# One attention kernel, fewer products against the maximum: key differences in a shared PSUM pair

## The chip, the cores and the metric

The program runs on one NeuronCore of a Trainium2 chip, in one launch. The metric is device time in microseconds (us) of one execution; less is better. In the rows PE is the matrix engine (PEld its weight loads), DVE the vector engine, ACT the scalar engine, POOL is GpSimd, and SP issues DMAs (SPq, ACTq: DMA issues on these queues).

## What is computed

Attention with queries averaged in pairs, then a gated layer and a soft mixture of experts. Cut to what matters here:

```python
# q, k, v: (4, 8, 1152, 64)
q_pool = q.reshape(B, H, S // 2, 2, D).mean(axis=3)          # 576 queries
scores = scale * np.matmul(q_pool, k.transpose(0, 1, 3, 2))  # 576 x 1152
scores = scores - np.max(scores, axis=-1, keepdims=True)
attn = np.exp(scores); attn = attn / (np.sum(attn, axis=-1, keepdims=True) + 1e-09)
attn_out = np.matmul(attn, v)
h = x @ w_in; x = (h * np.cos(h)) @ w_out                    # 2304 tokens, 512 -> 2048 -> 512
# then: logits, two softmaxes, 8 experts with 4 slots each, combined per token
```

The change touches the attention alone (and the moments at which some weights of the gated layer are decoded beside it).

## The kernel before

**Attention.** Two of the 32 heads make a pair; a pair fills the 128 partitions (64 per head). There are 16 pairs, and each has two units of 288 queries. A unit has nine score blocks, one for every 128 keys. A block t goes through these steps:

- *products* (L409): fp32 matmuls of the keys `kr` and pooled queries `qs` into a PSUM pair `s` (two banks, [128, 2, 512]), then *maxima* (L418): four bf16 matmuls of ones with `D`, a matrix that has minus the maximum of each query on its diagonals. They subtract the maximum from the scores in PSUM;
- *exp* (L423, ACT), from PSUM to an `e` buffer in SBUF;
- *av* (L431, PE): `e` times the values `vr`, added up over the nine blocks in the PSUM pair `o`;
- *add* (L440): `e` is added to a running sum, on DVE (letter V in `ADD_BY`) or on GpSimd (G). The first block of each letter is only the start. So a unit has three additions on DVE and four on GpSimd, and one (L443, DVE) that joins the two sums. Then `sums` (L511, PE), and a chain of small DMAs (L526, L536, L540), a reciprocal (L529) and a scaling on GpSimd (L543, L555).

The maxima come from a coarser product: 14 *rounds* per pair (L305, PE, bf16) into PSUM, each reduced by DVE (L310), then a small turn (L317), a last reduction (L324, L329) and nine diagonals on ACT (L343). They are made one pair ahead. Per pair SP loads `qr` (both queries of each average), `kr`, `vr`; DVE averages (L260, as a sum: the factor sits in the exponent's scale); ACT casts to bf16 (L263).

**PSUM.** Three pairs of banks (`BANKS = 3`) serve the score blocks, the rounds and the sums; a user takes whichever is free first. The fourth pair is `o`.

**Order.** Every step is entered into `Plan` with an engine, a duration and a due time; `Plan.order` lists them: each engine takes, of the steps that can start first, the one that is due first. Due times are multiples of `P` plus numbers of the tables `ROUNDS` and `DUES`. A step with `port=True` is kept from overlapping with another such step (DVE additions and GpSimd's work). So each engine's order is fixed when the program is built, and on the chip an engine waits at an instruction until its operands are there; nothing behind it passes.

Of the kernel before, what the change touches and what calls it, by code (L numbers as in the profile page):

```python
# [135 lines left out]
class Attention:  # L136
# [15 lines left out]
    ROUNDS = (-10.7, -8.2, -10.4, -9.8, -3.7, -4.8, -3.3, -0.8, -8.1, 0.5, 1.6, 2.2, 7.5, 7.7)
    FIRST_ROUNDS = (-13, -12, -11, -10, -9, -8, -7, -5, -7.2, -4.0, -2.3, -1.6, 0.9, 2.4)
    E_BUFS = 8

    BEHIND = 13.8
# [72 lines left out]
    def operands(self, p, m):  # L229
# [40 lines left out]
        for i, (a, n) in enumerate(q_parts):  # L270
            x = op(m + 0.5 * i, "SP", 0.6, lambda a=a, n=n: load_q(a, n), [first], uses=[("qr", p)],
                   more=4.2 if p else (2.4, 2.8, 3.3)[i], early=early)
            x = op(at_("pooled", 0.1 * i) if p else m, "V", 0.07 + n / 960, lambda a=a, n=n: pooled(a, n), [x], uses=[("qr", p), ("qs", p)], port=True)
# [1245 lines left out]
```

## Time and profile before

| what | us |
|---|---|
| runs: median (lowest, highest) of 3 | 871.1 (870.7, 872.5) |
| the profiled execution: its own time | 872.76 |
| its span, first to last instruction | 870.5 |
| attention, first round to last av | 7.5 to 398 |
| PE, DVE, ACT, POOL busy, share of the span | 97%, 81%, 61%, 45% |

The attention takes the first 45% of the span, the gated layer and the experts the rest. A busy share is an average over stages; matmul rows show modelled ends, so that what a group of matmuls costs is read from its start to the start of the next group. The granted TensorE clock is full (1.00) in all stretches of the attention.

### The profile page before, as it was taken

The page shows a single profiled execution, that of the slowest core. Times are in us where ns is not written, and L with a number is a line of the kernel's source. Part 1 is how long each engine was busy: PE and PEld are TensorE (multiplying, and loading weights), DVE is VectorE, ACT ScalarE, POOL GpSimd, SP SyncE. Part 2 cuts the span into 40 slices and gives each one's busy share as a digit, 9 for nine tenths or more (in the row PEclk, how much of TensorE's full clock was granted, in tenths as well). Part 3 has the DMA queues.
Part 4 walks back from the last instruction along what each step waited for, and adds up shares of the span by engine and source line. Part 5 has one row for each costly group of instructions (what it writes and reads, how often), then busy time and mean ns, then how long its engine had stood idle before and what let it go on. Part 6 is the DMA issues. An engine that isn't in the chain of part 4 may idle for free.

```text
span 870.5 us, 24363 instructions
## 1 busy us (share of the span) xinstructions
PE 847.4 (97%) x9901; PEld 612.2 (70%) x9901; DVE 704.2 (81%) x1309; ACT 527.7 (61%) x1132; POOL 390.6 (45%) x381
## 2 busy tenths in 40 slices
PE   5999999999999999999999999999999999999996
PEld 3666566656666666667788888888888888877355
DVE  6999999899899888855989888888899889544423
ACT  3777777767777777774875555555555555454223
POOL 0566656766666666664554333344433333220100
PEclk9999999999999999999999999999999999999898
DMA  7033323333333233111121111110111110594897
GB/s 254 15 94 113 112 74 90 98 106 101 101 101 88 80 101 101 46 44 44 54 61 50 36 37 49 49 48 29 49 49 49 38 36 13 226 422 151 317 423 227
DMA packets 53969, 90.89 MB, mean 104 GB/s; under 512 B 21473, under 2 KB 33505, under 8 KB 49761
## 3 DMA queue, kind: packets, MB, share of 16 engines
q1 hardware_dynamic: 53568, 88.76, 31.3%
q8 instruction: 77, 1.26, 0.6%
q10 hardware_dynamic: 288, 0.59, 0.2%
q14 instruction: 36, 0.29, 0.1%
HBM read 78.71 MB, written 4.72 MB: 96 GB/s over the span
## 4 chain that ended last, share of the span: by engine, by line
PE 91%; DVE 4%; ACT 2%; issue 1%; POOL 1%; DMA 1%; SPq 0%; DVEq 0%; ACTq 0%
PE ops L780 21%; PE hps L780 21%; PE o L431 16%; PE s L409 15%; PE m L305 4%; PE s L418 4%; PE hq L1341 2%; PE so L1384 2%; PE sums L511 1%; DVE mp L310 1%; PE xtp L961 1%; PE fo L1413 1%; DMA qr<-in_q_dram 1%; PE lgp L975 1%; PE sps L1160 1%
## 5 line engine op out<-in xcount | busy, mean ns | idle before, releaser
L310 DVE TENSOR_REDUCE mp<-m 128x2 f32<-128x768 f32 x224 | 203.6, 952 | 29.8 <-PE m L305 29.4
L423 ACT ACTIVATE e<-s 128x576 f32<-128x576 f32 x288 | 176.3, 653 | 53.2 <-PE s L418 50.7
L780 PE MATMUL ops<-w,g 128*128 128x512 f32 x864 | 206.3, 391 | 2.0 <-POOL g L818 1.4
L780 PE MATMUL hps<-x,w 128*128 128x512 f32 (+1 forms) x960 | 204.5, 368 | 0.0
L780 PEld LDWEIGHTS hps<-x,w 128*128 128x128 f32 x960 | 168.0, 188 | 31.7 <-issue 1.5
L780 PEld LDWEIGHTS ops<-w,g 128*128 128x128 f32 x864 | 160.7, 188 | 36.9 <-POOL g L818 2.4
L409 PE MATMUL s<-qs,kr 64*64 64x288 f32 x2304 | 180.5, 403 | 3.2 <-DVE mp L310 3.1
L431 PE MATMUL o<-e,vr 64*64 64x288 f32 x2304 | 181.0, 406 | 0.0
L818 POOL TENSOR_TENSOR g<-r,g 128x512 fp32r<-128x512 f32 (+1 forms) x80 | 100.1, 1252 | 147.3 <-ACT g L815 121.3
L440 POOL TENSOR_TENSOR acc<-acc,e 128x576 f32<-128x576 f32 x96 | 136.6, 1423 | 3.2 <-ACT e L423 0.9
L805 ACT ACTIVATE r<-r 128x512 f32<-128x512 f32 (+1 forms) x160 | 94.0, 587 | 69.4 <-DVE r L798 67.7
L440 POOL TENSOR_TENSOR acc<-e 128x576 f32<-128x576 f32 x32 | 48.5, 1517 | 153.5 <-ACT e L423 153.5
L409 PEld LDWEIGHTS s<-qs,kr 64*64 64x64 f32 x2304 | 79.7, 133 | 44.0 <-DVE mp L310 7.4
L431 PEld LDWEIGHTS o<-e,vr 64*64 64x64 f32 x2304 | 82.7, 133 | 31.8 <-issue 7.1
L741 POOL TENSOR_TENSOR da<-da,w 128x256 f32<-128x256 f32 x64 | 49.3, 771 | 94.6 <-DVE db L730 42.1
L418 PE MATMUL s<-D,a_ones 64*64 64x288 bf16 x1152 | 87.2, 283 | 0.0
L305 PE MATMUL m<-kb,qb 64*64 64x384 bf16 x896 | 74.0, 331 | 9.3 <-ACT qb L263 7.5
L798 DVE SCALAR_TENSOR_TENSOR r<-ki,hps 128x512 f32<-128x512 int32 (+1 forms) x80 | 50.4, 631 | 36.1 <-ACT ki L795 34.1
L815 ACT CAST g<-r 128x512 fp32r<-128x512 f32 (+1 forms) x80 | 46.2, 578 | 40.0 <-DVE r L808 37.5
L795 ACT ACTIVATE ki<-hps 128x512 int32<-128x512 f32 (+1 forms) x80 | 44.0, 551 | 39.1 <-PE hps L780 38.0
L941 DVE TENSOR_TENSOR acc<-acc,ops 128x512 f32<-128x512 f32 x70 | 47.7, 685 | 22.4 <-PE ops L780 22.4
L343 ACT ACTIVATE D<-a_minus,mc 128x64 bf16<-128x64 f32 x142 | 37.4, 336 | 33.1 <-DVE mc L324 32.9
(148 smaller groups left out, 952.5 us busy)
## 6 DMA issues: line engine op xcount, KB each, us to landing
raw<-in_w_io_dram SPq DMA_DIRECT2D x64, 256.0 KB
w1t<-in_w_dram SPq DMA_DIRECT2D x15, 1024.0 KB
vr<-in_v_dram SPq DMA_DIRECT2D x16, 576.0 KB
qr<-in_q_dram SPq DMA_DIRECT2D x15, 576.0 KB
kr<-in_k_dram SPq DMA_DIRECT2D x15, 576.0 KB
w2t<-in_w2b_dram SPq DMA_DIRECT2D x8, 1024.0 KB
r<-row SPq DMA_DIRECT2D x32, 144.0 KB
late<-in_w2a_dram SPq DMA_DIRECT2D x4, 1024.0 KB
```

Of the source, the lines that this page charges most:

```text
L305: nc.tensor.matmul(ps[heads[c], h.start // 64, 0:self.KC], w, m, start=True, stop=True)
L310: nc.vector.tensor_reduce(out=self.mp[p][:, x], in_=st[i][:, :, 0:self.KC], axis=AX.X, op=ALU.max)
L409: nc.tensor.matmul(ps[y:y + 64, h, 0:N], w, self.qs[p][x, s], start=True, stop=False)
L418: nc.tensor.matmul(ps[y:y + 64, h, 0:N], self.ones16[x], D[x, s], start=False, stop=True)
L423: nc.scalar.activation(out=st["e"], in_=st["ps"][:, :, 0:N], func=ACTF.Exp, scale=1.0 / 16.0)
L431: nc.tensor.matmul(self.o[u][64 * h:64 * h + 64, r, 0:N], self.vr[p][x, h, t], st["e"][x, h], start=(t == 0), stop=(t == J - 1),)
L440: self.engine(who).tensor_tensor(out=acc[who], in0=x, in1=st["e"], op=ALU.add)
L741: nc.gpsimd.tensor_tensor(out=st["a"], in0=st["a"], in1=fl(half(0)), op=ALU.subtract)
L780: nc.tensor.matmul(ps, x, y, start=(i == 0 and m == 0), stop=(i == n - 1 and m == 2))
L798: nc.vector.scalar_tensor_tensor(out=st["r"], in0=st["ki"], scalar=-c, in1=x, op0=ALU.mult, op1=ALU.add)
L805: nc.scalar.activation(out=st["r"], in_=st["r"], **kw)
L818: nc.gpsimd.tensor_tensor(out=g["l"][:, i], in0=st["r"], in1=fl(g["h"][:, i]), op=ALU.subtract)
```

## The change

- For pairs 1 to 15, blocks 0, 3, 4 and 8 of a unit (`CHAIN`) use one PSUM pair, one after the other. Block 0 is made as before, with the maxima. For the next ones a *link* (L433 in the changed kernel) adds the product of the queries with a *difference* of two key blocks to what stands in PSUM. The sum is then the next block's score, with the maximum already subtracted. So these three blocks have no maxima. A link waits until the exp of the block before it has read the PSUM pair.
- The differences are made in place in `kr` once per pair, by one subtraction over 384 columns on GpSimd (L307), after ACT has cast the keys.
- Key blocks are taken in another order (`block`), in score and av alike.
- Pooled queries of pairs 1 to 15: SP loads the first half into `qs`; GpSimd issues a DMA (L269) that adds the second half to it. DVE's averaging remains for pair 0 alone.
- Additions: three on DVE, three on GpSimd and one (the letter v) by a DMA that GpSimd issues (L478), which adds `e` to DVE's sum in SBUF. The sum's next addition on DVE (L480) waits for its landing.
- `e` has 10 buffers, before 8; `mp` 3, before 2; `qr` one, for pair 0.
- All tables of due times, `P` and the moments of the early weight decoding (`FIRST_FROM`, `FIRST_EVERY`) have other numbers.

The same steps in the changed kernel have other lines: products L446, maxima L455, link L433, rounds L330, av L468, exp L460, reductions L333, join L483, casts L275, scaling L589, low parts L601.

```diff
-    P = 1.28
+    P = 1.257
...
-    ADD_BY = "VVVGGGGVG"
...
+    ADD0 = "VVGvGGVGV"
+    ADD1 = "VVGvVGGVG"
...
+    ROUNDS = (-11.8, -8.8, -5.8, -13.6, -4.9, -18.8, -8.2, -1.7, -4.0, 6.6, -1.3, 6.6, 1.7, 8.7)
...
+    E_BUFS = 10
+    ISSUE, LANDING = 0.95, 5.5
+
+    BEHIND = 10.68
...
+        "load": -1.3, "free": -1.2, "v": 7.7, "pooled": 5.2, "qb": -13.0, "kb": -17.8, "top": -45.5,
...
+    CHAIN, DELTA_BY = (0, 3, 4, 8), "G"
...
-            self.qr[p] = self.two.tile([128, 2, NQ], FP32, tag="qr", name="qr")
+            if p == 0:
+                self.qr[p] = self.one.tile([128, 2, NQ], FP32, name="qr")
             self.kr[p] = self.three.tile([128, S], FP32, tag="kr", name="kr")
+            self.mp[p] = self.three.tile([128, sum(len(x) for x in self.rounds), 2], FP32, tag="mp", name="mp")
...
         def load_q(a, n):
-            nc.sync.dma_start(out=self.qr[p][:, :, a:a + n], in_=q[:, :, a:a + n])
+            if p:
+                nc.sync.dma_start(out=self.qs[p][:, a:a + n], in_=q[:, 0, a:a + n])
+            else:
+                nc.sync.dma_start(out=self.qr[p][:, :, a:a + n], in_=q[:, :, a:a + n])
...
         def pooled(a, n):
+            if p:
+                nc.gpsimd.dma_start(out=self.qs[p][:, a:a + n], in_=q[:, 1, a:a + n], accum_op=ALU.add)
+                return
...
+            if p:
+                x = op(at_("pooled"), "G", self.ISSUE, lambda a=a, n=n: pooled(a, n), [x], uses=[("qs", p)], port=False, more=self.LANDING)
...
+        if p:
+            n = 128 * (len(self.CHAIN) - 1)
+
+            def delta():
+                x = self.kr[p]
+                self.engine(self.DELTA_BY).tensor_tensor(out=x[:, 0:n], in0=x[:, 0:n], in1=x[:, 128:128 + n], op=ALU.subtract)
+
+            x = op(at_("delta"), self.DELTA_BY, (0.07 + n / 960, 0.08 + n / 447)[self.DELTA_BY == "G"], delta,
+                   sum([x for x in self.k_after[p].values()], []), uses=[("kr", p)], port=True, name="delta")
+            self.delta_after[p] = [x]
...
+        links = list(self.CHAIN) if p else []
+        others = [t for t in range(J) if t not in links]
+
+        def block(t):
+
+            return len(links) - 1 - links.index(t) if t in links else len(links) + others.index(t)
+
+        def link(t, st):
+            st["ps"] = ps = sts[links[0]]["ps"]
+            s, b = slice(N * c, N * c + N), 128 * block(t)
+            for h in range(2):
+                x = slice(64 * h, 64 * h + 64)
+                for y in (0, 64):
+                    w = self.kr[p][x, b + y:b + y + 64]
+                    out = ps[y:y + 64, h, 0:N]
+                    nc.tensor.matmul(out, w, self.qs[p][x, s], start=False, stop=True, skip_group_check=True)
...
+            s, b = slice(N * c, N * c + N), 128 * block(t)
             for h in range(2):
                 x = slice(64 * h, 64 * h + 64)
                 for y in (0, 64):
-                    w = self.kr[p][x, 128 * t + y:128 * t + y + 64]
+                    w = self.kr[p][x, b + y:b + y + 64]
...
+                        self.o[u][64 * h:64 * h + 64, r, 0:N], self.vr[p][x, h, block(t)], st["e"][x, h],
...
+            if by_dma:
+                nc.gpsimd.dma_start(out=acc[who], in_=st["e"], accum_op=ALU.add)
+                return
...
+            elif t in links[1:]:
+                ks = ("s", u, links[0])
+                x = es[links[links.index(t) - 1]]
+                a = op(s, "P", 0.486, lambda t=t, st=st: link(t, st), [x, *self.delta_after[p]], uses=[ks, *uses[:2]], name="scores")
...
-            who = self.ADD_BY[t]
+            who = (self.ADD0, self.ADD1)[c][t]
+            who, by_dma = who.upper(), who.islower()
...
+            by_dma &= not new
+            x = op(s + due["add"] * P, "G" if by_dma else who, self.ISSUE if by_dma else (0.667, 1.37)[who == "G"],
+                   lambda who=who, st=st, before=before, new=bool(new), by_dma=by_dma: add(who, st, before, new, by_dma), [e, last], new=new,
+                   uses=[ke] + ([("e", u, t0)] if new else [key]), port=not by_dma, more=self.LANDING * by_dma)
...
-FIRST_FROM, FIRST_EVERY, FIRST_DUE = 2.14, -0.96, 1000
+FIRST_FROM, FIRST_EVERY, FIRST_DUE = 4.04, -0.3, 1000
```

What that makes of the order. **PE, second unit of a late pair, its first score blocks.** Before, each block is products then maxima, and the wait at its head is for the pair of three blocks ago:

```order
L418 LDWEIGHTS a_ones_130
L418 MATMUL s<-D,a_ones_130 64x288
L409 MATMUL s<-qs,kr 64x288 [waits Activation_49]
L409 MATMUL s<-qs,kr 64x288 x3
L418 LDWEIGHTS a_ones_130
L418 MATMUL s<-D,a_ones_130 64x288
```

Now, after the third block (its last maxima are the first two rows) and then once more after a round and an av:

```order
L455 LDWEIGHTS a_ones_130
L455 MATMUL s<-D,a_ones_130 64x288
L433 MATMUL s<-qs,kr 64x288 [waits Activation_49]
L433 MATMUL s<-qs,kr 64x288 x3
L446 MATMUL s<-qs,kr 64x288 [waits Activation_49]
L446 MATMUL s<-qs,kr 64x288 x3
```

```order
L330 LDWEIGHTS qb
L330 MATMUL m<-kb,qb 64x384
L468 MATMUL o<-e,vr 64x288 [waits DVE_49]
L468 MATMUL o<-e,vr 64x288 x3
L433 MATMUL s<-qs,kr 64x288 [waits Activation_49]
L433 MATMUL s<-qs,kr 64x288 x3
L446 MATMUL s<-qs,kr 64x288 [waits Activation_49]
L446 MATMUL s<-qs,kr 64x288 x3
```

A link has no maxima, and the next block follows it at once, waiting for one of the two pairs that the chain leaves. Between the first link and the second stand one block, one round and one av.

**POOL, about one unit of a middle pair.** Before, four additions (`acc<-e` is a unit's first) with a scaling and its low parts between them:

```order
L440 TENSOR_TENSOR acc<-e 128x576 [waits Activation_49]
L440 TENSOR_TENSOR acc<-acc,e 128x576 [waits Activation_49,Pool_49]
L543 TENSOR_TENSOR xu<-xu,r 128x288 [waits DMAHW0_49]
L440 TENSOR_TENSOR acc<-acc,e 128x576 [waits Activation_49,Pool_49]
L555 TENSOR_TENSOR x_67<-xu,x_66 128x224 [waits Activation_49]
L555 TENSOR_TENSOR x_69<-xu,x_68 128x64 [waits Activation_49]
L440 TENSOR_TENSOR acc<-acc,e 128x576 [waits Pool_49]
```

Now:

```order
L269 DMA qs<-in_q_dram 128x576 [waits DMAHW3_49,DMASW4_49]
L478 DMA acc<-e 128x576 [waits DMASW5_49,DVE_49,Activation_49]
L480 TENSOR_TENSOR acc<-e 128x576 [waits Activation_49]
L589 TENSOR_TENSOR xu<-xu,r 128x288 [waits DMAHW5_49]
L307 TENSOR_TENSOR kr<-kr 128x384 [waits DMAHW4_49,Activation_49]
L480 TENSOR_TENSOR acc<-acc,e 128x576 [waits Activation_49,Pool_49]
L601 TENSOR_TENSOR x_69<-xu,x_68 128x288 [waits Activation_49]
L480 TENSOR_TENSOR acc<-acc,e 128x576 [waits Pool_49]
```

One addition has become a DMA issue at the unit's start, and in every second unit a query DMA and the key differences came in ahead of the additions.

**DVE, from the end of a unit into the next one.** Before:

```order
L260 TENSOR_TENSOR qs<-qr 128x576 [waits DMAHW0_49]
L502 TENSOR_TENSOR xu<-xu,o 128x288 [waits Activation_49]
L440 TENSOR_TENSOR acc<-acc,e 128x576 [waits DVE_49]
L443 TENSOR_TENSOR acc<-acc 128x576 [waits DVE_49,Pool_49]
L440 TENSOR_TENSOR acc<-e 128x576 [waits Activation_49]
L440 TENSOR_TENSOR acc<-acc,e 128x576 [waits DVE_49,Activation_49]
L529 RECIPROCAL fold<-fold 128x36 [waits DMAHW6_49,DMAHW7_49,DMAHW1_49,DMAHW0_49]
```

Now:

```order
L548 TENSOR_TENSOR xu<-xu,o 128x288 [waits Activation_49]
L480 TENSOR_TENSOR acc<-acc,e 128x576 [waits DMASW3_49]
L764 TENSOR_SCALAR da<-da 128x256
L480 TENSOR_TENSOR acc<-acc,e 128x576 [waits DVE_49]
L480 TENSOR_TENSOR acc<-e 128x576 [waits Activation_49]
L483 TENSOR_TENSOR acc<-acc 128x576 [waits DVE_49,Pool_49]
L333 TENSOR_REDUCE mp<-m 128x2 [waits PE_49]
```

The averaging is gone, and the addition behind the join of `xu` now waits for the landing of the DMA that was issued in the unit before.

## Rows read from the trace of the kernel before

**Rows 1.** The page's head, busy times, and chain of work that ended last.

```profile
span 870.5 us, 24363 instructions
PE 847.4 (97%) x9901; PEld 612.2 (70%) x9901; DVE 704.2 (81%) x1309; ACT 527.7 (61%) x1132; POOL 390.6 (45%) x381
PE 91%; DVE 4%; ACT 2%; issue 1%; POOL 1%; DMA 1%; SPq 0%; DVEq 0%; ACTq 0%
```

**Rows 2.** Waits of PE from 30 to 380 us: total, times, longest.

```profile
PE s L409 <- DVE mp L310: 2.8, 2, 1.4
```

**Rows 3.** Timeline: start, us, engine, line, operation; score blocks, rounds, av, sums, turn.

```profile
202.93 0.34 PE L305 MATMUL m<-kb,qb 64*64 64x384 bf16 x4
203.09 1.15 PE L431 MATMUL o<-e,vr 64*64 64x288 f32 x16
204.06 0.51 PE L305 MATMUL m<-kb,qb 64*64 64x384 bf16 x8
...
207.80 0.67 PE L409 MATMUL s<-qs,kr 64*64 64x288 f32 x8
208.28 0.30 PE L418 MATMUL s<-D,a_ones 64*64 64x288 bf16 x4
208.41 0.66 PE L409 MATMUL s<-qs,kr 64*64 64x288 f32 x8
...
211.44 0.67 PE L409 MATMUL s<-qs,kr 64*64 64x288 f32 x8
...
218.48 0.45 PE L511 MATMUL sums<-acc,a_ones 128*32 128x144 f32 x8
...
241.72 0.45 PE L511 MATMUL sums<-acc,a_ones 128*32 128x144 f32 x8
```

**Rows 4.** Windows, 100 to 350 us: busy PE, PEld, DVE, ACT, POOL, granted clock.

```profile
100.00:350.00 250.00, 247.25 (x4754) 156.18 (x4750) 226.53 (x351) 182.86 (x413) 157.44 (x142) 1.00 0.33 96
```

**Rows 5.** Groups of instructions, 100 to 350 us: busy, mean ns of one.

```profile
L440 DVE TENSOR_TENSOR acc<-acc,e 128x576 f32<-128x576 f32 x43 | 36.3, 845 | 0.5
L260 DVE TENSOR_TENSOR qs<-qr 128x576 f32<-128x576 f32 x11 | 8.2, 748 | 0.0
L440 POOL TENSOR_TENSOR acc<-acc,e 128x576 f32<-128x576 f32 x64 | 90.3, 1411 | 1.8 <-ACT e L423 0.5
L543 POOL TENSOR_TENSOR xu<-xu,r 128x288 f32<-128x288 f32 x21 | 16.7, 797 | 0.0
```

**Rows 6.** Timeline: two exps in a row on ACT.

```profile
208.75 1.20 ACT L423 ACTIVATE e<-s 128x576 f32<-128x576 f32 x2
```

**Rows 7.** Timeline of the program's start.

```profile
0.74 0.40 SPq L707 DMA_DIRECT2D raw<-in_w_io_dram  x1
1.20 1.98 SPq L249 DMA_DIRECT2D qr<-in_q_dram  x3
6.80 0.29 DVE L260 TENSOR_TENSOR qs<-qr 128x128 f32<-128x128 f32 x1 [5.07 <-DMA qr<-in_q_dram]
8.06 0.96 DVE L310 TENSOR_REDUCE mp<-m 128x2 f32<-128x768 f32 x1 [0.30 <-PE m L305]
9.07 0.54 PE L305 MATMUL m<-kb,qb 64*64 64x384 bf16 x4 [0.33 <-DVE mp L310]
9.27 7.87 DVE L310 TENSOR_REDUCE mp<-m 128x2 f32<-128x768 f32 x9
17.05 0.16 DVE L324 TENSOR_REDUCE mc<-m 128x4 f32<-128x12 f32 x1
```

**Rows 8.** Timeline: a DMA from SBUF to SBUF, and who waits for it.

```profile
391.35 0.57 SPq L540 DMA_DIRECT2D r<-row  x1
393.80 0.81 POOL L543 TENSOR_TENSOR xu<-xu,r 128x288 f32<-128x288 f32 x1 [0.67 <-DMA r<-row]
```

**Rows 9.** Timeline around the first of PE's two waits of Rows 2.

```profile
104.01 1.52 POOL L440 TENSOR_TENSOR acc<-e 128x576 f32<-128x576 f32 x1 [2.38 <-ACT e L423]
104.17 1.97 DVE L440 TENSOR_TENSOR acc<-acc,e 128x576 f32<-128x576 f32 x1
105.39 0.30 PE L418 MATMUL s<-D,a_ones 64*64 64x288 bf16 x4
106.07 1.81 DVE L310 TENSOR_REDUCE mp<-m 128x2 f32<-128x768 f32 x2
107.07 0.72 PE L409 MATMUL s<-qs,kr 64*64 64x288 f32 x8 [1.38 <-DVE mp L310]
```

More of the change, by code (lines that the diff above doesn't have):

```diff
@@ L136 @@
 class Attention:
-    P = 1.28
+    P = 1.257
     QB, KC = 64, 384
-    ADD_BY = "VVVGGGGVG"
[L152 to L156, printed above, removed]
+    ADD0 = "VVGvGGVGV"
+    ADD1 = "VVGvVGGVG"
+    ROUNDS = (-11.8, -8.8, -5.8, -13.6, -4.9, -18.8, -8.2, -1.7, -4.0, 6.6, -1.3, 6.6, 1.7, 8.7)
+    FIRST_ROUNDS = (-13, -12, -11, -75.4, -55.3, -30.0, -21.7, -13.1, -10.2, -6.2, -1.9, 1.7, 2.6, 6.4)
+    E_BUFS = 10
+    ISSUE, LANDING = 0.95, 5.5
+    BEHIND = 10.68
     DUES = {
-        "load": 1.4, "free": 4.4, "v": 23.6, "pooled": 11.1, "qb": 3.0, "kb": -23.2, "top": -45.4,
-        "diagonal": 50.2, "add": 31.2, "whole": -30.9, "take": -41.6, "join": -9.5, "sums": 14.9, "out": -15.9,
-        "fold": -26.2, "inv": -14.5, "row": 30.0, "spread": 13.4, "scale": -2.4, "high": 65.4, "low": 18.3,
+        "load": -1.3, "free": -1.2, "v": 7.7, "pooled": 5.2, "qb": -13.0, "kb": -17.8, "top": -45.5,
+        "diagonal": 43.4, "add": 30.2, "whole": -48.8, "take": -32.1, "join": -58.3, "sums": 13.8, "out": -3.2,
+        "fold": -47.9, "inv": 12.4, "row": 51.1, "spread": 23.8, "scale": -12.2, "high": 70.4, "low": 49.9,
+        "delta": -7.2,
     }
+    CHAIN, DELTA_BY = (0, 3, 4, 8), "G"
     JOIN_BY, SCALE_BY, LOW_BY = "V", "G", "G"
@@ L265, in operands @@
         ring = lambda names, size: [(n, size, (n, p)) for n in names]
-        new = ring(["kr", "qs"], 3) + ring(["qr", "qb", "kb"], 2)
+        new = ring(["kr", "qs", "mp"], 3) + ring(["qb", "kb"], 2)
         first = op(m, "SP", 0.0, tiles, new=new, early=early)
@@ L270, in operands @@
         for i, (a, n) in enumerate(q_parts):
[L271 removed]
+            x = op(m + 0.5 * i, "SP", 0.6, lambda a=a, n=n: load_q(a, n), [first], uses=[("qs", p)],
                    more=4.2 if p else (2.4, 2.8, 3.3)[i], early=early)
[L273 removed]
+            if p:
+                x = op(at_("pooled"), "G", self.ISSUE, lambda a=a, n=n: pooled(a, n), [x], uses=[("qs", p)], port=False, more=self.LANDING)
+            else:
+                x = op(m, "V", 0.07 + n / 960, lambda a=a, n=n: pooled(a, n), [x], uses=[("qs", p)], port=True)
             self.s_after[p].append(x)
@@ L307, in reduce @@
         def reduce(i, x):
-            if i == 0:
-                self.mp[p] = self.two.tile([128, sum(size), 2], FP32, tag="mp", name="mp")
             nc.vector.tensor_reduce(out=self.mp[p][:, x], in_=st[i][:, :, 0:self.KC], axis=AX.X, op=ALU.max)
@@ L431, in av, with add @@
                     nc.tensor.matmul(
-                        self.o[u][64 * h:64 * h + 64, r, 0:N], self.vr[p][x, h, t], st["e"][x, h],
+                        self.o[u][64 * h:64 * h + 64, r, 0:N], self.vr[p][x, h, block(t)], st["e"][x, h],
                         start=(t == 0), stop=(t == J - 1),
                     )
-        def add(who, st, before, new):
+        def add(who, st, before, new, by_dma=False):
             x = acc[who] if before is None else before["e"]
@@ L477, in half_of @@
             before = sts[t0] if count == 1 else None
-            x = op(s + due["add"] * P, who, (0.667, 1.37)[who == "G"],
-                   lambda who=who, st=st, before=before, new=bool(new): add(who, st, before, new), [e, last], new=new,
-                   uses=[ke] + ([("e", u, t0)] if new else [key]), port=True)
+            by_dma &= not new
+            x = op(s + due["add"] * P, "G" if by_dma else who, self.ISSUE if by_dma else (0.667, 1.37)[who == "G"],
+                   lambda who=who, st=st, before=before, new=bool(new), by_dma=by_dma: add(who, st, before, new, by_dma), [e, last], new=new,
+                   uses=[ke] + ([("e", u, t0)] if new else [key]), port=not by_dma, more=self.LANDING * by_dma)
             where[who] = (count + 1, t, x)
```

6 lines of the change are left out of this document (2 added, 4 removed).

## The prediction

> **What bounds the kernel now.** I read the chain of work that ended last first: 91% of it is PE [rows 1]. So a change in the attention counts only by what it takes from PE's queue there, or by what PE has to wait for. The second view is PE's own waits from 30 to 380 us: one line, two waits, 2.8 us in all [rows 2]. PE is packed. The timeline says with what: the sums of the same unit of neighbouring pairs stand at 218.48 and 241.72, so a pair takes 23.24 us [rows 3]. Inside it, from start to start: six score blocks from 207.80 to 211.44, 0.607 us each, of which products are 0.48 and maxima 0.12 to 0.13 (0.607 - 0.485 = 0.122); a round 203.09 - 202.93 = 0.16; two avs 204.06 - 203.09 = 0.97, so 0.485 each [rows 3]. 18 blocks, 18 avs and 14 rounds make 10.9 + 8.7 + 2.2 = 21.9 us; sums, turns and changes between kinds are the other 1.3. Nothing in 23.24 is left for waiting.
>
> The others are close behind. Over 100 to 350 us, 250 / 23.24 = 10.76 pairs, DVE is busy 226.5, ACT 182.9 and POOL 157.4 us [rows 4]: 21.05, 17.0 and 14.6 us of a pair's 23.24.
>
> **Maxima that go.** Three blocks of nine lose them, in 30 units (pairs 1 to 15): 90 x 0.122 = **10.9 us** off PE, with the packed queue closing up. A pair's PE work becomes 23.24 - 0.73 = 22.5 us, a unit's 11.25.
>
> **What the links wait for.** The chain keeps one of three PSUM pairs for most of a unit, so rounds, sums and the other five blocks share two. From the end of a block it takes 0.34 us until its exp starts (the products at 208.41 follow a block; its exp starts at 208.75), 0.65 for the exp [rows 3, 6] (1.20 for two in a row, so 0.55 from one to the next), and some 0.05 until PE goes on (a reduction from 8.06 to 9.02 lets PE start at 9.07 [rows 7]). So a pair comes back 1.04 us after its block. Before, two blocks lie between, 2 x 0.607 = 1.21: 0.17 to spare. Now the block after the first link needs the second block's pair, with one block and one link between: 0.607 + 0.485 = 1.09, 0.05 to spare. The second link needs the exp of the first; a block, a round and an av lie between: 0.607 + 0.16 + 0.485 = 1.25. ACT lags by another 0.05 after four exps in a row, so it needs 1.1: 0.15 to spare. The order thus fits by some hundredths. I take 0.05 us of new waiting a unit, **+1.5 us**; from 0 (the margins hold) to +6 (two or three places a unit late by 0.08).
>
> **DVE.** Pair by pair it loses the averaging, 0.75 us [rows 5], and keeps its three additions a unit. 21.05 - 0.75 = 20.3 of 22.5, 90%, as before (21.05 of 23.24, 91%). It is no bound and gives PE nothing; 0.
>
> **POOL.** It loses two additions a pair, 2 x 1.41, and gets the differences over 384 columns: between 0.80 (288 columns) and 1.41 (576), about 1.0 [rows 5]. 14.6 - 2.8 + 1.0 = 12.8 us, so 9.7 of a pair are free for three DMA issues. No POOL issue is in the trace; the nearest is SP's, 0.57 us [rows 8]. Up to 3.2 us each POOL keeps up, so 0. The differences are needed by the next pair's first link and stand a unit ahead of it; hidden, and if they came late PE would wait for the excess once a pair.
>
> **The accumulating DMAs.** The trace has none. A plain DMA within SBUF of 144 KB lands 2.45 us after its issue begins (391.35, awaited until 393.80 [rows 8]), the first query load from HBM at most 5.6 us after (1.20 to 6.80 [rows 7]). I take 4, nearer to the row within SBUF, since `e` has 288 KB. The room: the addition is issued when the fourth exp of a unit is done, some 3.4 us after the unit's first block (the link starts after three blocks, 1.82, ends 2.31, then 0.34, 0.65 and a lag of 0.05). DVE's waiting addition stands behind the join of `xu`, about 1.1 us into the next unit. 11.25 + 1.1 - 3.4 = 8.9 us. With an issue of 1 us, 7.9 are left for a landing of 2.45 to 5.6: hidden, 0. What is queued behind that addition on DVE: two more additions, the join of the sums and the next rounds' reductions, which give PSUM pairs back to PE. So an excess goes straight to PE. The query DMA has five exps' time of a unit at least, 5/9 x 11.25 = 6.2 us; hidden too.
>
> The Trainium skill bears on this: "DMA: Bandwidth & Descriptors", Anatomy of one DMA, fits a DMA issued from GpSimd as about 2.0 us plus bytes over 436,000 per us. For 294,912 bytes that is an estimate of 2.7 us, within my bounds; the sum stays the same by it. It tells nothing of accumulation.
>
> **The shared port.** Both of PE's waits are of one kind [rows 9]: POOL begins an addition at 104.01; DVE's, begun at 104.17, takes 1.97 us where its mean is 0.85 [rows 5], the reduction behind it is late, and PE stands 1.38 us. From the maxima at 105.39 to the next products it is 1.68 us where 0.13 is usual, so 1.55 lost each, 3.1 in the two. POOL's operand work falls from 14.6 to 12.8 us a pair, DVE's two-operand work by the averaging, but the margin of the PSUM pairs is smaller. I keep the 3.1 us as they are: 0, from -3.1 to +10.5 (below).
>
> The Trainium skill's rule for this is in "SBUF — State Buffer", Who interferes with whom: a DVE instruction with two SBUF inputs and a GpSimd one that reads SBUF exclude each other, and the second waits for the whole first. The trace agrees: 104.01 + 1.52 = 105.53, and DVE ends at 106.14. The rule speaks against the differences, one more reader on POOL, 15 times 1.0 us; if every one met an addition and found no slack, it would be +15 us. It gives the rival "port" its mechanism.
>
> **The start.** Now queries and keys are loaded ahead of the weights (raw at 0.74, queries from 1.20 [rows 7]), so the first queries can land up to 0.46 us sooner or a little more. Nine reductions instead of ten stand ahead of the first `mc` at 17.05: 0.95 us. DVE sets the pace there (7.87 us for nine in a row). I take **-1.0**, from 0 to -2.0.
>
> After the attention no step changes; the layers behind start earlier by the gain.
>
> **Sum**, against the profiled execution's own 872.8: -10.9 + 1.5 + 0 - 1.0 = -10.4, 862.4. The median of the runs is 871.1, 1.7 under that execution; so **860.7**. The ends: -10.9 - 3.1 - 2.0 = -16.0 gives 855.1; -10.9 + 6 + 3.1 (two more port waits) = -1.8 gives 869.3.
>
> **Rivals.**
> 1. *Pairs too few.* Exps or reductions land 0.1 us later than I read at two places a unit: 0.2 x 30 = 6, no gain at the start: 871.1 - 10.9 + 6 = 866.2. For it: margins of 0.05. Against: the orders before had 0.17 and PE's matmuls show no wait for ACT [rows 2]. At 0.36 us a unit the gain is gone.
> 2. *Port.* DVE additions blocked by POOL find less slack, and every second pair has a wait of 1.4 us: 7.5 x 1.4 = 10.5, and 871. Then the maxima are gone and the time stays: it doesn't do what it is built for. From eight such waits on. For it: two cases of exactly this [rows 9]. Against: POOL works 12.8 instead of 14.6 us a pair with operands.
> 3. *Slower: the landing.* An accumulating DMA that lands over 7.9 us after its issue makes DVE stand in every unit, with the reductions behind it. At 9.5 us: 1.6 x 30 = 48, minus 10.4, so 908. It decides from 7.9 + 0.35 = 8.3 us. For it: accumulating reads the target too, and no row shows one. Against: 2.45 and 5.6 us of plain ones.
> 4. *Better.* No waits at all: 871.1 - 10.9 - 3.1 - 1.0 = 856.1.
>
> **How the numbers follow.** Forecast (856.5 to 864): 0.50. Pairs too few (864 to 869.4): 0.20. Better: 0.06. Port or any other tie: 0.10. Landing: 0.14. The range 855 to 869.5 holds the first two and most of the third, about 0.75 to 0.8; with both signs apart, the forecast's own is 856.5 to 864. A measurement of this kernel tells 0.2% (1.7 us) from no change. Faster 0.76, within 0.2% 0.10, slower 0.14.
>
> **What would show it.** Right: sums of neighbouring pairs 22.5 to 22.7 us apart; 792 maxima matmuls instead of 1152; DVE's L480 with no wait for a DMA; POOL under 100%. Rival 1: PE waits for ACT e or DVE mp ahead of L446 and L433. Rival 2: DVE's L480 has a mean over 0.9 us, PE waits of 1.4. Rival 3: DVE L480 waits for DMA `acc`, in every unit. The prediction is wrong if PE's pair keeps over 23.1 us, or if something behind the attention moves.

## The result, and the profile after

The changed kernel takes 860.46 us (median of 4 runs, 858.45 to 863.79) where the kernel before takes 871.11 (870.71 to 872.5): a ratio of 0.988, 95% interval 0.9845 to 0.9913. Forecast were 860.7, from 855.0 to 869.5. The time came out within 0.3 us, and that is partly luck: a gain of 3.8 us that the sum had left out stands against some 3.5 us of losses that it had left out too.

The page's head, the busy times and the chain of work of the profiled execution (its own time is 858.45). PE has 360 matmuls fewer than before (9541 instead of 9901), the 1152 - 792 of the forecast:

```profile
span 856.7 us, 23690 instructions
PE 837.0 (98%) x9541; PEld 605.4 (71%) x9541; DVE 691.0 (81%) x1294; ACT 528.7 (62%) x1132; POOL 398.3 (46%) x411
PE 91%; DVE 4%; DMA 1%; ACT 1%; issue 1%; SPq 0%; POOL 0%; DVEq 0%; ACTq 0%
```

PE's waits from 30 to 380 us, the view of [rows 2]; then the timeline's sums of the same unit of two neighbouring pairs, as in [rows 3]:

```profile
PE sums L557 <- DVE acc L483: 0.5, 1, 0.5
PE m L330 <- DVE mp L333: 0.4, 1, 0.4
PE s L446 <- ACT r L564: 0.3, 1, 0.3
...
210.21 0.45 PE L557 MATMUL sums<-acc,a_ones 128*32 128x144 f32 x8
...
232.81 0.45 PE L557 MATMUL sums<-acc,a_ones 128*32 128x144 f32 x8
```

232.81 - 210.21 = 22.60 us a pair, and eleven pairs in a row have just this. Before, by the sums of first units, 23.23 was usual, but three pairs took 25.33, 25.33 and 24.00, each right behind one of 22.75 to 22.80; the two PE waits of [rows 2] lie in the first two of these. So before, an average pair had 23.50.

The window from 100 to 350 us and the groups in it, as [rows 4, 5]:

```profile
100.00:350.00 250.00, 250.00 (x4693) 157.56 (x4688) 224.52 (x355) 191.42 (x431) 169.18 (x170) 1.00 0.54 124
...
L480 POOL TENSOR_TENSOR acc<-acc,e 128x576 f32<-128x576 f32 x44 | 68.6, 1559 | 0.9
L480 DVE TENSOR_TENSOR acc<-acc,e 128x576 f32<-128x576 f32 x46 | 34.6, 752 | 0.0
L478 POOL DMA_DIRECT2D acc<-e x22 | 19.1, 870 | 60.7 <-ACT e L460 59.0 <-ACT kb L275 1.7
L307 POOL TENSOR_TENSOR kr<-kr 128x384 f32<-128x384 f32 x11 | 14.5, 1321 | 0.0
L269 POOL DMA_DIRECT2D qs<-in_q_dram x10 | 9.0, 905 | 14.5 <-DVE mp L333 5.9 <-DVE xu L548 4.6 <-DMA qs<-in_q_dram 4.0
```

DVE's additions have 752 ns instead of 845: in this window none is held up any more. POOL's seem to have become slower, 1559 ns instead of 1411. That is a trap of reading, as the timeline of one unit shows. POOL first:

```profile
212.05 0.88 POOL L269 DMA_DIRECT2D qs<-in_q_dram  x1 [1.16 <-DMA qs<-in_q_dram]
215.58 0.87 POOL L478 DMA_DIRECT2D acc<-e  x1 [2.65 <-ACT e L460]
216.15 1.75 POOL L480 TENSOR_TENSOR acc<-e 128x576 f32<-128x576 f32 x1
217.52 1.12 POOL L589 TENSOR_TENSOR xu<-xu,r 128x288 f32<-128x288 f32 x1
218.27 1.32 POOL L307 TENSOR_TENSOR kr<-kr 128x384 f32<-128x384 f32 x1
219.23 1.73 POOL L480 TENSOR_TENSOR acc<-acc,e 128x576 f32<-128x576 f32 x1
220.59 1.11 POOL L601 TENSOR_TENSOR x<-xu,x 128x288 fp32r<-128x288 f32 x1
221.34 1.72 POOL L480 TENSOR_TENSOR acc<-acc,e 128x576 f32<-128x576 f32 x1
```

The addition at 216.15 is shown with 1.75 us, yet the next instruction starts at 217.52, 1.37 later; the differences take 219.23 - 218.27 = 0.96, not 1.32. From start to start a POOL addition costs 1.37 us in both kernels (1.36 before, from 99.46 to 100.82). The same stretch on DVE:

```profile
212.75 0.75 DVE L480 TENSOR_TENSOR acc<-acc,e 128x576 f32<-128x576 f32 x1
...
223.64 0.75 DVE L480 TENSOR_TENSOR acc<-acc,e 128x576 f32<-128x576 f32 x1
...
225.85 0.75 DVE L483 TENSOR_TENSOR acc<-acc 128x576 f32<-128x576 f32 x1
```

The two engines take turns: POOL's instructions with operands run from 216.15 to 222.7 (221.34 + 1.37), DVE's additions from 223.64 to 226.6. Only POOL's DMA issues lie beside DVE additions, that at 212.05 for its last 0.18 us, and they delay none. In another pair an issue covers a whole addition, which keeps its 0.75 us (POOL, then DVE):

```profile
122.36 1.04 POOL L269 DMA_DIRECT2D qs<-in_q_dram  x1 [1.90 <-DVE mp L333]
...
122.35 0.75 DVE L480 TENSOR_TENSOR acc<-acc,e 128x576 f32<-128x576 f32 x1
```

The accumulating DMA issued at 215.58 is awaited by the addition at 223.64, 8.06 us later. Its landing (DMA to landing, min/median/max, of L478):

```profile
DMA to landing us min/median/max: 3.4/4.5/6.5
```

DVE's waits from 30 to 380 us have one for such a landing, in the last pair, where the addition at 366.95 starts 4.51 us after the issue at 362.44:

```profile
DVE acc L480 <- DMA acc<-e: 2.0, 1, 2.0
```

Where the time went, by the profiled executions: 14.3 us between them (872.76 and 858.45), 10.65 between the medians. The first sums come 0.76 us earlier (40.33 to 39.57); the 14 pairs from there lose 12.5: 14 x 0.63 = 8.8 by the steady pair and 3.8 by the uneven ones of before. The end of the attention gives 0.8 back (in the last units two DVE additions of 1.23 and 1.97 us), so the last av comes 12.5 earlier (397.55 to 385.06). The gated layer and what follows then differ mostly by the granted clock. Windows of the kernel before, then of the changed one:

```profile
815.00:820.00 5.00, 3.77 (x20) 2.03 (x20) 2.95 (x7) 0.41 (x1) 0.00 (x0) 0.69 0.56 210
820.00:825.00 5.00, 5.00 (x32) 1.15 (x28) 1.95 (x4) 0.27 (x1) 2.19 (x4) 0.62 0.71 256
```

```profile
405.00:410.00 5.00, 2.89 (x10) 1.73 (x9) 5.00 (x11) 4.67 (x10) 2.41 (x3) 0.94 0.19 52
410.00:415.00 5.00, 5.00 (x18) 3.96 (x17) 5.00 (x12) 3.88 (x8) 2.03 (x2) 0.72 0.19 52
...
804.00:809.00 5.00, 3.77 (x29) 1.66 (x32) 3.34 (x8) 0.68 (x1) 0.00 (x0) 1.00 0.70 261
```

Early in the gated layer PE now stands 2.1 us in two waits close together, and then the granted clock falls, to 0.94 and 0.72 of full in these two windows (0.50, the level of 1.2 GHz, from 410 to 412); the gated layer ends only 10.8 us earlier. Before, PE stood there nearly as long, 2.0 us in three waits of 0.7 between 418 and 430, and the clock stayed at 1.00. At the end it is the other way: PE has the same 1.2 us of idle time in both kernels, but the clock falls only in the profiled execution of the one before, and 3.0 us of the 14.3 lie there. The four runs of the changed kernel have mean granted clocks from 0.991 to 0.994, so the clock differs from execution to execution, and the medians are the fair measure.

### The profile page after: what moved, and what is told of

It is laid out like the page before. It is cut to its first block, busy times and chain, and to the rows that moved or that the text cites. A ratio compares the mean times of both kernels' runs of the same rounds, so it can differ in the third digit from the quotient of the medians.

```text
span 856.7 us, 23690 instructions
## 1 busy us (share of the span) xinstructions
PE 837.0 (98%) x9541; PEld 605.4 (71%) x9541; DVE 691.0 (81%) x1294; ACT 528.7 (62%) x1132; POOL 398.3 (46%) x411
## 3 DMA queue, kind: packets, MB, share of 16 engines
q8 instruction: 75, 1.23, 0.6%
## 4 chain that ended last, share of the span: by engine, by line
PE 91%; DVE 4%; DMA 1%; ACT 1%; issue 1%; SPq 0%; POOL 0%; DVEq 0%; ACTq 0%
PE ops L827 22%; PE hps L827 22%; PE o L468 16%; PE s L446 10%; PE s L433 5%; PE m L330 4%; PE s L455 3%; DVE mp L333 2%; PE so L1431 2%; PE hq L1388 2%; PE sums L557 1%; PE xtp L1008 1%; DVE acc L480 1%; PE fo L1460 1%; PE lgp L1022 1%
## 5 line engine op out<-in xcount | busy, mean ns | idle before, releaser
L333 DVE TENSOR_REDUCE mp<-m 128x2 f32<-128x768 f32 x224 | 205.2, 948 | 26.0 <-PE m L330 23.8
L460 ACT ACTIVATE e<-s 128x576 f32<-128x576 f32 x288 | 174.6, 650 | 44.8 <-PE s L455 26.6
L468 PE MATMUL o<-e,vr 64*64 64x288 f32 x2304 | 179.0, 407 | 0.0
L446 PE MATMUL s<-qs,kr 64*64 64x288 f32 x1584 | 128.5, 405 | 0.7 <-DVE mp L333 0.3
L468 PEld LDWEIGHTS o<-e,vr 64*64 64x64 f32 x2304 | 81.9, 133 | 31.8 <-issue 6.8
L480 POOL TENSOR_TENSOR acc<-acc,e 128x576 f32<-128x576 f32 x64 | 99.2, 1550 | 2.2 <-ACT e L460 1.0
L788 POOL TENSOR_TENSOR da<-da,w 128x256 f32<-128x256 f32 x64 | 51.3, 801 | 95.5 <-DVE db L777 42.7
L330 PE MATMUL m<-kb,qb 64*64 64x384 bf16 x896 | 76.2, 331 | 8.0 <-ACT qb L275 6.2
L446 PEld LDWEIGHTS s<-qs,kr 64*64 64x64 f32 x1584 | 55.2, 132 | 34.1 <-ACT e L460 8.5
L478 POOL DMA_DIRECT2D acc<-e x32 | 27.9, 872 | 87.9 <-ACT e L460 79.3
L455 PE MATMUL s<-D,a_ones 64*64 64x288 bf16 x792 | 59.9, 283 | 0.0
L433 PE MATMUL s<-qs,kr 64*64 64x288 f32 x720 | 59.8, 402 | 0.0
```

Of the source, the lines that this page charges most:

```text
L330: nc.tensor.matmul(ps[heads[c], h.start // 64, 0:self.KC], w, m, start=True, stop=True)
L333: nc.vector.tensor_reduce(out=self.mp[p][:, x], in_=st[i][:, :, 0:self.KC], axis=AX.X, op=ALU.max)
L433: nc.tensor.matmul(out, w, self.qs[p][x, s], start=False, stop=True, skip_group_check=True)
L446: nc.tensor.matmul(ps[y:y + 64, h, 0:N], w, self.qs[p][x, s], start=True, stop=False)
L455: nc.tensor.matmul(ps[y:y + 64, h, 0:N], self.ones16[x], D[x, s], start=False, stop=True)
L460: nc.scalar.activation(out=st["e"], in_=st["ps"][:, :, 0:N], func=ACTF.Exp, scale=1.0 / 16.0)
```

## The experiments

Four of the eleven kernels keep the changed kernel's order (the three whose names say so, and late_landing). In the others the planner lists it anew, in four of them with due times searched anew, and all of these are slower than the changed kernel. So those that keep its order weigh most. The larger number of `e` and `mp` buffers and the new tables were not tried apart.

**same_order_maxima**: the maxima back, in place.

```diff
             def delta():
-                x = self.kr[p]
-                self.engine(self.DELTA_BY).tensor_tensor(out=x[:, 0:n], in0=x[:, 0:n], in1=x[:, 128:128 + n], op=ALU.subtract)
+                pass
...
-                    nc.tensor.matmul(out, w, self.qs[p][x, s], start=False, stop=True, skip_group_check=True)
+                    nc.tensor.matmul(out, w, self.qs[p][x, s], start=True, stop=False)
+            maxima(t, st)
```

> The changed kernel with its order word for word, but what stands in a link's place is a full block: products of the raw keys (no differences are made) and four maxima matmuls behind them, in the same shared PSUM pair. So 90 times the maxima are back and nothing else moves but POOL's 0.96 us a pair of differences, which are left out. Theory (the maxima's work is the gain): pairs of 22.60 + 6 x 0.12 to 0.13 = 23.3 us, 860.5 + 10.5 to 11.5 = 871 to 872 us, and a bit over if the slower PE shifts DVE's and POOL's instructions into each other. Rival (much of the gain is the relief of DVE and POOL): pairs well under 23.2 us, 867 us or less.

870.58 us (868.41 to 873.0, 10 runs), 0.9994 of before (0.9979 to 1.0008). Pairs of 23.34, even from 85 to 354 us. So the maxima's work is 6 x 0.123 = 0.74 us a pair, 15 x 0.74 = 11.1 by the pairs and 10.1 by the medians. With the rest of the change in place the whole gain is there; the rival falls. The rest of the change, without the chain, stands where the kernel before stood. That does not make the rest idle: the next two kernels keep the chain and lose more than the gain without one of the DMAs.

**same_order_pool_add**: the accumulating DMA becomes an addition on POOL, in place.

```diff
-                nc.gpsimd.dma_start(out=acc[who], in_=st["e"], accum_op=ALU.add)
+                nc.gpsimd.tensor_tensor(out=acc[who], in0=acc[who], in1=st["e"], op=ALU.add)
```

> The changed kernel with its order word for word on all engines, but each accumulating DMA of e is a plain addition on POOL to the same sum (1.37 us where the issue took 0.87; the chain and the query DMA stay). Theory 1 (the addition by DMA is what keeps POOL out of DVE's way: adds_pool had an addition of 1.97 us on DVE in every pair): DVE instructions of about 2 us in most units, pairs of 23.5 us or more, 870 to 885 us. Theory 2 (adds_pool suffered from its own order): pairs of 22.6 to 22.8 us and 859 to 863 us.

880.75 us (4 runs), 1.0109 of before (1.0074 to 1.0144): 20 us worse than the changed kernel for half a microsecond more of POOL a unit, 15 us in all. PE's waits from 30 to 380 us, and one DVE step beside POOL's new addition:

```profile
PE m L330 <- DVE mp L333: 15.4, 16, 2.3
```

```profile
167.95 1.80 POOL L478 TENSOR_TENSOR acc<-acc,e 128x576 f32<-128x576 f32 x1 [2.43 <-DVE acc L480]
```

```profile
168.40 1.63 DVE L791 TENSOR_TENSOR w<-da,db 128x256 fp32r<-128x256 f32 x1
169.96 0.94 DVE L333 TENSOR_REDUCE mp<-m 128x2 f32<-128x768 f32 x1
```

L791 needs 0.42 us elsewhere; here it stands until POOL's addition is through, the reduction behind it is late, and PE with it. Pairs of 23.5 to 24.1, and an early one of 27.6. Theory 1 holds, in the decoding steps and in additions of 1.1 us rather than in additions of 2 us.

**same_order_pool_avg**: the query's second half added by POOL in the place of its DMA issue (`qr` in two buffers for all pairs, loaded whole).

```diff
-                nc.gpsimd.dma_start(out=self.qs[p][:, a:a + n], in_=q[:, 1, a:a + n], accum_op=ALU.add)
-                return
...
-            nc.vector.tensor_tensor(
+            (nc.gpsimd if p else nc.vector).tensor_tensor(
```

> The changed kernel with its order of steps on all engines, but the second query half is not added by a DMA: both halves are loaded to a buffer, and POOL adds them in the place of its DMA issue (about 1.37 us where the issue took 0.88). In the changed kernel that issue stands at 212.05 us, and DVE's additions of 0.75 us begin at 212.75, beside it, with no delay. Theory (an addition on POOL holds what DVE's addition needs, an issue does not): DVE's first addition of every second unit takes 1.3 to 2 us, what follows on DVE is 0.6 to 1.2 us later, and PE pays 0 to 1.2 us a pair: pairs of 22.6 to 23.8 us, 861 to 878 us. Rival (only POOL's own time counts, and POOL is idle there): DVE's additions stay at 0.75 us and the time at 859 to 862 us.

873.37 us (870.3 to 875.36, 10 runs), 1.0015 of before (0.9999 to 1.0032); pairs of 23.2 to 23.7. POOL, then DVE:

```profile
218.98 1.45 POOL L265 TENSOR_TENSOR qs<-qr 128x576 f32<-128x576 f32 x1 [1.67 <-DMA qr<-in_q_dram]
```

```profile
219.03 2.01 DVE L473 TENSOR_TENSOR acc<-acc,e 128x576 f32<-128x576 f32 x1
```

The issue stood beside the same addition without harm; POOL's addition costs DVE's 1.26 us. PE waits 8.4 us for reductions, in 13 places. The rival falls: 13 us, though POOL was idle there.

**all_maxima** and **maxima_late_decode**: a chain of one block, order listed anew; the second also with the weight decoding late.

```diff
-    P = 1.257
+    P = 1.28
...
-    CHAIN, DELTA_BY = (0, 3, 4, 8), "G"
+    CHAIN, DELTA_BY = (0,), "G"
...
-FIRST_FROM, FIRST_EVERY, FIRST_DUE = 4.04, -0.3, 1000
+FIRST_FROM, FIRST_EVERY, FIRST_DUE = 13.5, 0.1, 1000
```

(The last edit is in maxima_late_decode alone.)

> The changed kernel with a chain of one block: all nine blocks of a unit have their maxima again, no links, no key differences; the accumulating DMAs, the buffers and the tables stay (P is 1.28 again). My theory (the gain is the maxima's work gone from a packed PE): the steady pair gets 0.73 us of maxima back and loses the 0.10 us that it has above the 22.5 us of counted work, so 22.60 + 0.63 = 23.23 us, and 15 x 0.63 = 9.5 on top of 860.5: 870. Rival (relief: the gain comes from DVE and POOL getting out of each other's way, since the two uneven pairs of 25.33 us of the kernel before follow DVE additions of 1.97 us): pairs of 22.8 us or less and a time of 864 or less. Whichever holds, DVE additions over 0.85 us between 60 and 360 us would mean that the relief alone does not remove the blocked additions; none of them would mean that it does, and is worth the 3.8 us that the uneven pairs of before cost.

881.42 us (872.94 to 883.69, 10 runs), 1.0091 of before: undisturbed pairs of 23.30, as the theory says, but 11 us above its time; four waits of PE for reductions make 9.1 us. No DVE addition between 60 and 360 us takes over 0.8 us, so the blocked additions are gone without the chain; what is blocked here are decoding steps. DVE, POOL and PE around 70 us:

```profile
69.58 5.09 DVE L764 TENSOR_SCALAR da<-da 128x256 f32<-128x256 f32 x1
```

```profile
69.20 0.88 POOL L478 DMA_DIRECT2D acc<-e  x1 [4.61 <-ACT e L460]
69.82 1.10 POOL L589 TENSOR_TENSOR xu<-xu,r 128x288 f32<-128x288 f32 x1
70.58 1.69 POOL L480 TENSOR_TENSOR acc<-e 128x576 f32<-128x576 f32 x1
71.94 1.22 POOL L601 TENSOR_TENSOR x<-xu,x 128x224 fp32r<-128x224 f32 x2
72.83 1.67 POOL L480 TENSOR_TENSOR acc<-acc,e 128x576 f32<-128x576 f32 x1
```

```profile
75.59 0.70 PE L446 MATMUL s<-qs,kr 64*64 64x288 f32 x4 [4.53 <-DVE mp L333]
```

A decoding step of 0.29 us is late by 4.8: five POOL instructions follow one another without a pause, and DVE's gets in only behind the last, at 74.4. Three more cases of 2.1 us follow at 123.0, 171.8 and 220.9, each behind one POOL addition.

> The kernel all_maxima with one line changed: the early weight decoding is due in the last three pairs of the attention, in no pair before. all_maxima had undisturbed pairs of 23.30 us, and in others four DVE steps of the decoding that took 2.1 to 5.1 us where 0.29 is usual, each right behind a DMA issue of POOL and beside POOL's next additions; PE stood 9 us behind them. Theory (blocked decoding steps made all_maxima's uneven pairs): the pairs from the third to the twelfth are all 23.3 us, and the time is 866 to 872, by how much the late decoding delays the gated layer; against the changed kernel's 860.5 and its 15 x 0.7 = 10.5 us for the maxima that is 871. Rival (the uneven pairs are a matter of the order with nine maxima): pairs of 24.4 us stay, 876 us or more.

882.08 us (4 runs). The pairs from the third to the tenth are 23.30 each, so the decoding made the uneven ones there, as the theory says. The eleventh has 24.86, though no decoding step is near: a join on DVE takes 1.98 us at 289.0, beside POOL's scaling. The time was missed: the last av starts at 392.6, 5.0 earlier than before, but then PE stands 9.3 us in one wait for ACT, and the granted clock falls to half. Windows behind the attention:

```profile
405.00:410.00 5.00, 0.00 (x0) 0.00 (x0) 4.23 (x10) 0.90 (x2) 1.88 (x3) 0.72 0.29 55
410.00:415.00 5.00, 1.22 (x2) 0.50 (x2) 2.32 (x3) 3.66 (x8) 2.34 (x3) 0.50 0.25 83
```

**before_moments**: the kernel before, with the changed kernel's moments of decoding.

```diff
-FIRST_FROM, FIRST_EVERY, FIRST_DUE = 2.14, -0.96, 1000
+FIRST_FROM, FIRST_EVERY, FIRST_DUE = 4.04, -0.3, 1000
```

> The kernel before with one line changed: the moments of the early weight decoding are those of the changed kernel. In the kernel before, the uneven pairs (25.33, 25.33 and 24.00 us where 23.23 is usual) are those in which DVE has two steps of the decoding between its additions, and an addition right behind them runs into one of POOL's. Theory (the place of the decoding decides which DVE instruction meets POOL): other pairs are uneven, or none; with none it is 871.1 - 3.8 = 867.3 us, with as many 871. Rival (the additions collide by themselves): the same three pairs stay uneven, 870.5 to 871.7.

873.55 us (872.32 to 874.59, 10 runs), 1.0024 of before (1.0015 to 1.0034). The uneven pairs moved: DVE additions of 1.97 us stand at 80.0, 151.1, 222.4 and 293.6, before at 104.2 and 175.5. One of them (DVE, then POOL), right behind a decoding step, as at 104.17 before:

```profile
150.10 0.75 DVE L440 TENSOR_TENSOR acc<-e 128x576 f32<-128x576 f32 x1
150.77 0.41 DVE L744 TENSOR_TENSOR w<-da,db 128x256 fp32r<-128x256 f32 x1
151.10 1.97 DVE L440 TENSOR_TENSOR acc<-acc,e 128x576 f32<-128x576 f32 x1
...
150.94 1.51 POOL L440 TENSOR_TENSOR acc<-e 128x576 f32<-128x576 f32 x1 [2.38 <-ACT e L423]
```

So the place of the decoding decides in which pair a DVE addition meets POOL's; these moments alone help nothing.

**average_dve**, **adds_pool** and **chain_alone**: the query averages on DVE; the addition by DMA on POOL; both. The chain stays, due times anew.

```diff
-                nc.gpsimd.dma_start(out=self.qs[p][:, a:a + n], in_=q[:, 1, a:a + n], accum_op=ALU.add)
-                return
...
-    ADD0 = "VVGvGGVGV"
-    ADD1 = "VVGvVGGVG"
+    ADD0 = "VVGVGGGGV"
+    ADD1 = "VGVVVGGGG"
```

(The first edit is that of average_dve, the second that of adds_pool; chain_alone has the first, and other strings with as many letters of each kind. The strings of average_dve are in another order, too.)

> The changed kernel with the query averages of all pairs on DVE, as before (0.75 us a pair), instead of the accumulating DMA that POOL issues; due times found anew for that. My theory (DVE is no bound at 20.3 of 22.6 us, nor at 21.05): pairs of 22.6 to 22.7 us and 859 to 863 us, the same as the changed kernel. Rival (DVE is the next bound, and the averaging is one more instruction that POOL can block): PE waits for DVE's reductions, pairs of 22.9 us or more, 865 us or more.

869.15 us (865.77 to 872.19, 10 runs), 0.9973 of before. Between disturbances pairs are 22.60 to 22.76, with 20.3 + 0.75 = 21.05 us of counted work on DVE: it is no bound. The rival's time came all the same, but by decoding steps that POOL blocks, not by the averaging: L756 takes 2.78 us at 137.8, 208.4 and 278.6 and 3.91 at 57.1, and PE waits 9.1 us for reductions. In the last of these pairs the clock also falls (0.82 and 0.84 from 280 to 290): 26.59 us, where the same stall of PE, 2.1 us, at full clock made 24.97.

> The changed kernel with the accumulating DMA of e replaced by a fourth addition on POOL in each unit (0.87 us of issue out, 1.37 us of addition in, so POOL has 1.0 us more a pair); the query DMA and the chain stay; due times found anew. Theory 1 (POOL has room): undisturbed pairs of 22.6 us and 859 to 864 us. Theory 2 (the addition by DMA is what keeps DVE and POOL apart): DVE instructions that take 2 us and more in some pairs, these pairs 24 us and more, 866 us or more.

878.59 us (4 runs), 1.0089 of before, pairs of 23.65 to 23.79, and in each an addition on DVE like this one:

```profile
196.60 1.97 DVE L479 TENSOR_TENSOR acc<-acc,e 128x576 f32<-128x576 f32 x1
```

Theory 2. Here the planner knew of the addition and kept its time free of others by its own durations, and it is still 18 us above the changed kernel.

> The changed kernel with its chain, but without the two kinds of accumulating DMAs: queries averaged on DVE as before, a unit's additions three on DVE and four on POOL as before; due times found anew for that. Theory 1 (the maxima's work carries the gain; DVE and POOL keep up, but sometimes get in each other's way): most pairs 22.6 us, some of 24 to 25, 862 to 869 us. Theory 2 (relief: without it the chain brings nothing): hardly a pair under 23.2 us, 870 us or more. Theory 3 (the DMAs bring nothing of their own): all pairs 22.6 us, 859 to 862 us.

890.85 us (4 runs), 1.0219 of before. The joins (L472) have a mean of 1286 ns where 752 is usual, the averages 1305, pairs are 23 to 25. Theory 2, in this order: the chain without the DMAs brings less than nothing.

**late_landing**: three plain copies ahead of each accumulating DMA, same order.

```diff
             if by_dma:
...
+                for x in self.spare:
+                    nc.gpsimd.dma_start(out=x, in_=st["e"])
                 nc.gpsimd.dma_start(out=acc[who], in_=st["e"], accum_op=ALU.add)
```

> The changed kernel with three plain copies of e (288 KB each, into spare buffers) issued on POOL's queue right ahead of each accumulating DMA of e; the order of all else is the same. So the accumulating DMA is issued 3 x 0.87 = 2.6 us later, and its queue has three transfers to do first. In the changed kernel the last packet lands 3.0 to 6.2 us after the issue (median 4.1) and the addition on DVE that waits for it starts 7.9 to 8.9 us after: 2.5 to 5.3 us to spare. My theory (hidden, but with a cliff: an excess goes to DVE and from there to PE): the landing moves by 2.6 us and by some 1 us more for each copy, 5.6 us in all, so it is late by 0.3 to 3 us in every unit; DVE's L480 waits for the DMA in most units, DVE's 2.3 idle us a pair take up part, and the time is 870 to 895 us. Rival (the additions have far more room than the trace shows, since DVE could do other work first): no wait of L480 for the DMA and 860 to 863 us. A second rival is POOL: 5.2 us more of issues a pair make its additions late, seen as waits of DVE's join for POOL.

896.9 us (4 runs), just above my theory's 895, but for another reason. DVE's waits from 30 to 390 us:

```profile
DVE fold L579 <- DMA fold<-r: 35.8, 13, 5.4
DVE mp L333 <- PE m L330: 17.5, 35, 1.8
DVE acc L484 <- DMA acc<-e: 2.0, 4, 0.7
```

The additions wait for the DMA only 2.0 us in all, no more than in the changed kernel, with a median landing of 6.8 us; and no wait of the join for POOL is among them, so the second rival falls. What is late are the sums on their way to the reciprocal, brought by four DMAs of 4.5 KB (`fold<-r`): 35.8 us of waiting on DVE (7.9 in the changed kernel), with the reductions behind, and PE waits 10.7 us for those at the turns (L340). Most of it arises ahead of these DMAs' issue, on SP, here after sums at 250.52:

```profile
253.31 0.58 SPq L590 DMA_DIRECT2D r<-row  x1
253.99 2.64 SPq L576 DMA_DIRECT2D fold<-r  x4
```

The issues of `fold<-r` begin 3.47 us after the sums, behind that of `r<-row`, which had to wait for the DMAs `row<-fold` of the unit before (18.4 us of such waits on SP, 7.0 in the changed kernel). Where DVE waits, the issues begin 1.2 to 4.8 us after the sums (0.8 to 1.7 in the changed kernel); from there to the reciprocal it is 5.2 to 8.2 us (5.7 to 6.9). So the big transfers hurt first through the small ones, which wait for one another in SP's queue. What makes `row<-fold` late was not traced further.

**five_chain**: one block more in the chain, due times anew.

```diff
-    CHAIN, DELTA_BY = (0, 3, 4, 8), "G"
+    CHAIN, DELTA_BY = (0, 2, 4, 6, 8), "G"
```

> The changed kernel with five blocks in the chain instead of four (so five blocks of nine have the maxima) and due times found anew; differences over 512 columns instead of 384. Theory 1 (maxima count, links do not wait): PE's work falls by another 2 x 0.123 = 0.25 us a pair, undisturbed pairs of 22.35 us, 857 to 860 us. Theory 2 (a link more is one wait for an exp more, with two pairs for all other blocks): PE waits for ACT's e ahead of links, pairs over 22.6 us, 861 to 868 us. As in the other kernels with a new order, DVE instructions that POOL blocks may lie on top: they show as DVE instructions of 1 to 2 us and PE waits for the reductions.

867.05 us (865.54 to 868.0, 7 runs). PE's waits for exps are 0.6 us in all, so theory 2 falls: links do not wait. Theory 1's 22.35 is not confirmed either: the pairs are between 19.8 and 29.3 in this order, with DVE steps held up to 3.93 us (L790 at 153.7). Whether four links can pay stays open. No kernel here beats the changed one.

## Why the prediction was right, and where it was not

- **Bound.** PE's queue is what counts: held. With PE even and full, 0.74 us of work a pair shows as 0.74 (same_order_maxima).
- **Maxima**, -10.9: right. 11.1 by the pairs, 10.1 by the medians.
- **Links' waiting**, +1.5: right in size, wrong in kind. The pair is 22.60 where 22.5 was counted, 15 x 0.10 = 1.5, but PE waits for no exp. From start to start the 14 rounds of a pair take 2.49 us instead of 2.39, products 8.78 instead of 8.73, avs 8.89 instead of 8.97: other neighbours in the queue. same_order_maxima, without any link, has the 2.49 too. So 0.05 us of margin held, and rival 1 did not come.
- **DVE**, 0: right, 224.5 us in 250 are 20.3 a pair; average_dve shows that 21.05 fit too, between its disturbances.
- **POOL**, 0: right in size (issues of 0.87 and 0.90, differences of 0.96 us), but for a reason that the prediction did not see. It counted POOL's operand work, 12.8 instead of 14.6 us. What matters is where each instruction stands: the two DMAs are worth 20 and 13 us in this order, since an issue does not hold up DVE and an addition does.
- **Accumulating DMAs**, hidden: right, but for 2.0 us of DVE's waiting in the last pair. Landing 4 us forecast, 4.5 measured; the upper bound of 5.6 was passed once or more (6.5). Room 8.9 forecast, 8.06 in the unit shown. Rival 3's point of 8.3 us was not reached. That an excess goes straight to PE by the waiting addition is not how it went in late_landing.
- **Port**, 0: this step failed. It said that the 3.1 us of blocked additions stay; they went, with 0.7 more that the waits view did not show (3.8 by the pairs). all_maxima has none of them either between 60 and 360 us, so they did not go by the chain; which of the other edits removed them is not shown apart, but each DMA that becomes an addition of POOL's brings blocked DVE instructions back. The range had the -3.1 as its lower end. Rival 2 came only at the attention's end here, but in most kernels with another order. The differences, for which the prediction named a bound of +15 us, met no addition: they stand at 218.27, DVE's additions at 223.64.
- **Start**, -1.0: 0.76 by the first sums. The first maxima came 2.36 earlier (18.75 to 16.39), and 1.6 of that was lost by 40 us.
- **"After the attention no step changes"**: no step did, but its time did, and by the prediction's own sign ("if something behind the attention moves") this part failed. In the profiled execution 12.5 us less at the last av are 10.8 at the end of the gated layer, with the PE stall of 2.1 us and the fall of the clock at 405 to 415. If all executions gain the 12.5 us in the attention, the medians lose 1.9 of them behind it; the others were not profiled, so this stays open.
- **The sum**: -10.65 instead of -10.4, in part by luck. The port gave 3.8 us more than forecast. Against it stand the start (0.2 less), the last pair, which is no steady one (0.6), the attention's end (0.8) and what lies behind it (1.9).

## What to carry over

- When two engines exclude each other, count not only the work of each but where each instruction stands. An edit of 0.5 us a unit on POOL, 15 us in all on an engine that is idle half of the time, cost 20 us, because it fell beside DVE's steps; a DMA issue in the same place held up none of them.
- To weigh one part of a change whose order is a planner's, edit the instruction in place and keep the order. Kernels with an order listed anew were up to 30 us off, much of it through collisions of their own.
- Read the cost of an instruction from start to start; a mean duration that rises may be a matter of the record.
